# Transposes of a fused attention and feed-forward kernel moved three steps later; layer one issued one step ahead at edges without scores

## The chip, the cores and the metric

The kernel runs on one core of a Trainium2 chip. The metric is the device time of one execution in microseconds (us), as a median of several runs; one execution was also recorded by the hardware profiler, and all rows below are of that one.

## The reference

Agent attention, then a feed-forward block on its output, all in float32 (B = 2, N = 12480, C = 128, 49 agents, 2048 hidden units):

```
s(a, b)  = softmax(a @ b.T / sqrt(128))        # row maximum taken off first, 1e-9 added to the sum
agent_v  = s(agents, k) @ v                    # 49 x 128
x        = s(q, agents) @ agent_v              # 12480 x 128, for each batch
h        = x @ w_in                            # 24960 x 2048
g        = where(h > 0, h, exp(min(h, 0)) - 1)
out      = g @ w_out                           # 24960 x 128
```

## The kernel before

agent_v is folded into the first weight matrix: A = agent_v @ w_in, so h = s(q, agents) @ A, with a contraction of only 49. A prologue converts the weights and does batch 0's half of the attention over the keys; it takes the first 55 us. The rest is one long loop over S = 416 **steps**.

A **round** is 960 tokens (26 rounds, numbered from 0) and 16 steps; a **half round** is 480 tokens and 8 steps, one for each 256 hidden units. Below, n is the step's place in its round, 0 to 15. The work of a step s:

- Layer one, `p1(s)` (L404, matmuls at L412): six matmuls in three pairs (a pair shares the array) into an `h` tile of two PSUM banks. `h` tiles come from `slot()` (L136), a pool of **three** that is used in turn. A slot can be written again when the last reader of its tile is done.
- The activation, `elu(s)` (L415): ScalarE takes relu(-h) (L418) and an exponential (L421); VectorE makes g (L423), the last reader of `h`.
- `split(s)` (L426), in four of the eight steps of a half round (c = 1, 4, 6, 7): VectorE casts g to hi (L430), GpSimd subtracts for lo (L207, 128x480, twice). In the other four steps g is multiplied as plain float32.
- Layer two, `p2(s)` (L436, matmuls at L452), four steps later (LAG = 4): adds g times w_out to two PSUM banks `o0` and `o1`, of which there is one each. After the eighth product of a half round both are copied out: VectorE copies o1 to `ob` (L464), ScalarE copies o0 to `oa` (L467), GpSimd adds them (L468) and a DMA stores the sum (L469). The next half round's first product, one step later, needs both banks.

The order on each engine is written out by hand: in step s first p1(s), then p2(s-4), then the elu of s with the `oa` copy between its two ScalarE instructions, then split(s), then whatever `at(step, function)` hung on the step. An engine does its instructions in that order. Since layer two trails by four steps, its half rounds end at n = 3 and n = 11 and begin at n = 4 and n = 12; these are the **edges**.

Attention for the queries of round j is hung on earlier steps (L620 to L635, s0 from `EDGE` = 3): at n = 11 two rounds ahead the 64 small score matmuls (L293), into a slot of their own, with maximum, subtraction, exponential and normalisation in the steps behind; then `q_ring(j)` (L355), at n = 3 of the round before j: eight transposes on TensorE (L334) into a slot of their own, a ScalarE copy (L348) and a VectorE subtraction (L207, 113x480) out of it as `px`, and four DMAs that copy the two `px` tiles to `py` with their halves swapped (L352, L353). SyncE's queue issues them, and then at n = 4 the load of later queries (L124). So each round has one edge with transposes (n = 3) and one with scores (n = 11). Rounds 24 and 25 have no scores to make, and round 25 has no transposes.

Batch 1's attention over its keys is spread over rounds 0 to 12: score rounds in rounds 0 to 6 (at n = 13 and n = 1); in rounds 7 to 11 a VectorE subtraction `e_sub` (L211) at n = 4, 8 and 12, an exponential `e_exp` (L214) a step later, and matmuls at n = 8, 12 and 0; at n = 4 of round 7 one small matmul with a slot; at n = 14 of round 11 and n = 2, 6 and 10 of round 12 matmuls `A_pe` (L262), each with a slot.

Of the kernel before, what the change touches and what calls it, by code (L numbers as in the profile page):

```python
# [24 lines left out]
def tile_agent_attention_moe(  # L25
# [21 lines left out]
    S = B * NG * NM  # L47
    LAG = 4
    WARM = 2
    LEAD = 6  # L50
    NP = NM // 2
# [84 lines left out]
    def slot(dt=F32):  # L136

        return ps_h.tile([128, 2, 512], dt, tag="h", name="h")
# [258 lines left out]
    h_t, e_t, g_t, hi_t, lo_t, o_t = {}, {}, {}, {}, {}, {}  # L397

    def at_step(s):

        x, c = divmod(s, NP)
        return x // 2, x % 2, c

    def p1(s):  # L404
        j, half, c = at_step(s)
        h = slot()
        ah, al = A[j // NG, c]
        hi, lo = p_t[j]
        for i, (a, p) in enumerate([(ah, hi), (ah, lo), (al, hi)]):
            for u, r in enumerate(ROWS):  # L410
                x = slice(r, r + NA)
                nc.tensor.matmul(out=h[:, u, 0:T], lhsT=a[x, :], rhs=p[u ^ half][x, :], start=i == 0, stop=i == 2)  # L412
        h_t[s] = h[:, :, 0:T]

    def elu(s, between=None):  # L415

        h, e = h_t.pop(s), x_p.tile([128, 2, T], F32, tag="e", name="e")
        nc.scalar.activation(out=e, in_=h, func=ACTF.Relu, scale=-1.0)  # L418
        if between:
            between()  # L420
        nc.scalar.activation(out=e, in_=e, func=ACTF.Exp, scale=-1.0)  # L421
        g = g_p.tile([128, 2, T], F32, tag="g", name="g", bufs=5)
        nc.vector.scalar_tensor_tensor(out=g, in0=e, scalar=-1.0, in1=h, op0=ALU.add, op1=ALU.max)  # L423
        g_t[s] = g

    def split(s):  # L426
        if at_step(s)[2] not in SPLIT:
            return
        hi_t[s] = g_p.tile([128, 2, T], F32R, tag="hi", name="hi", bufs=3)
        nc.vector.tensor_copy(out=hi_t[s], in_=g_t[s])  # L430
        lo_t[s] = []
        for i in range(2):
            lo_t[s].append(g_p.tile([128, T], F32R, tag=f"lo{i}", name=f"lo{i}", bufs=3))
            rest(nc.gpsimd, lo_t[s][i], g_t[s][:, i, :], hi_t[s][:, i, :])
# [42 lines left out]
    def at(s, fn, *a):  # L477
        pre.setdefault(s, []).append((fn, a))

    with tc.manual_schedule():  # L480
# [137 lines left out]
        o_p = ctx.enter_context(tc.tile_pool(name="o", bufs=1))  # L618

        groups[0] = 32  # L620
        for j in range(1, B * NG):
            s0 = (j - 1) * NM + EDGE
            if j + 1 < B * NG:
                at(s0 + 1, load_q, j + 1)
            if j > 1:
                s0 -= NP
            at(s0, q_scores, j)
            at(s0, q_max)
            at(s0, q_sub)
            at(s0 + 1, q_exp)  # L630
            at(s0 + 2, q_sum)
            at(s0 + 2, q_rz, 0)
            at(s0 + 3, q_rz, 1)
            at(s0 + 4, q_mul)
            at(s0 + (9 if j == 1 else NP), q_ring, j)  # L635
        def k_round(r):
            ps = attn_bank()
            scores_pe(ps, k_t.pop((1, r)), 1, 0, R)
            k_out(ps, r)

        for r in range(NR):
            s0 = (r // 2) * NM + 13 + 4 * (r % 2)
# [8 lines left out]
        for r in range(NR):  # L651
            s0 = (7 + r // 3) * NM + 8 + 4 * (r % 3)
# [9 lines left out]

        for s in range(S + LAG):
            after = None
            if s < S:
                p1(s)
            if s == 2:
                t = ps_o.tile([128, 512], F32, tag="o0", name="o0")
                for _ in range(2):
                    nc.tensor.matmul(out=t[:, 0:T], lhsT=ident, rhs=win_sb[:, 0:T], start=True, stop=True)  # L670
            x = s - LAG + (s < LEAD)
            if x >= 0 and s != LEAD:
                after = p2(x)
            if s < S:
                elu(s, after)
                split(s)
            elif after:
                after()
            for fn, a in pre.pop(s, []):
                fn(*a)  # L680
# [34 lines left out]
```

## Time and profile before

| | |
|---|---|
| median of 3 runs | 1029.28 us (1029.2 to 1029.38) |
| the profiled execution | 1029.82 us, its span 1028.0 us |
| TensorE | busy 1004.7 us, 98% |
| ScalarE | busy 896.5 us, 87% |
| VectorE | busy 816.3 us, 79% |
| GpSimd | busy 587.3 us, 57% |
| mean granted TensorE clock | 0.998 |

Busy time counts an instruction from its start to its modelled end. A matmul's end is modelled, so gaps of TensorE are better seen from the distance between starts than from busy time. The timeline names, for each instruction or run of like instructions, start and length in us, engine, line, operation, tiles, shapes and count, and in brackets the idle time before it with what ended it. Two matmuls of a pair stand as two rows with nearly one start.

### The profile page before, as it was taken

What the parts mean: (1) busy time and instruction counts of PE and PEld (TensorE: products, weight loads), DVE (VectorE), ACT (ScalarE), POOL (GpSimd) and SP (SyncE); (2) the same over time, 40 slices, a digit from 0 to 9 for tenths busy, and PEclk for the clock granted to TensorE, in tenths of its full rate; (3) what the DMA queues carried; (4) which work ended last, traced back from release to release, by engine and by line L of the source; (5) the groups of instructions that cost most, each with busy time, mean ns of one, the idle gap of its engine ahead of it and who ended that gap; (6) DMA issues with size and microseconds to landing.
All of it is one profiled execution on the core that took longest, in us unless ns stands there. A gap on an engine that the chain in (4) does not pass through costs nothing.

```text
span 1028.0 us, 24953 instructions
## 1 busy us (share of the span) xinstructions
PE 1004.7 (98%) x10242; PEld 752.6 (73%) x10242; DVE 816.3 (79%) x989; ACT 896.5 (87%) x1018; POOL 587.3 (57%) x490
## 2 busy tenths in 40 slices
PE   7899999999999999999999999999999999999998
PEld 5767777777776677777766777777777777777796
DVE  7778788788888777887778888878887887888775
ACT  4588998998898888888889999999999999999995
POOL 3236565565565565566555565656656565656655
PEclk9999999999999999999999999999999999999999
DMA  9911211211222322320110111011011101101000
GB/s 349 376 72 45 93 64 37 86 64 45 78 64 71 90 65 60 101 64 11 54 45 11 54 45 44 22 54 44 21 44 45 54 11 54 45 26 40 26 20 20
DMA packets 25980, 67.27 MB, mean 65 GB/s; under 512 B 3083, under 2 KB 14963, under 8 KB 25867
## 3 DMA queue, kind: packets, MB, share of 16 engines
q1 hardware_dynamic: 25867, 65.69, 19.2%
q8 instruction: 80, 1.31, 0.5%
q14 instruction: 33, 0.27, 0.1%
HBM read 43.11 MB, written 12.78 MB: 54 GB/s over the span
## 4 chain that ended last, share of the span: by engine, by line
PE 85%; DVE 6%; ACT 5%; issue 2%; DMA 1%; POOL 0%; SPq 0%; POOLq 0%; DVEq 0%; ACTq 0%
PE o L452 53%; PE h L412 26%; DVE g L423 3%; ACT e L421 3%; PE h L293 2%; PE h L222 1%; PE h L159 1%; ACT e L418 1%; DMA k<-in_kT_dram 1%; DVE m_all L168 0%; ACT s_all L214 0%; ACT ex L102 0%; DVE ex L106 0%; PE h L262 0%; DVE fr L108 0%
## 5 line engine op out<-in xcount | busy, mean ns | idle before, releaser
L207 POOL TENSOR_TENSOR lo<-g,hi 128x480 fp32r<-128x480 f32 x416 | 512.4, 1254 | 391.2 <-DVE hi L430 229.5
L423 DVE SCALAR_TENSOR_TENSOR g<-e,h 128x960 f32<-128x960 f32 x416 | 478.5, 1152 | 174.8 <-ACT e L421 140.6
L418 ACT ACTIVATE e<-h 128x960 f32<-128x960 f32 x416 | 403.5, 970 | 59.5 <-PE h L412 48.9
L421 ACT ACTIVATE e<-e 128x960 f32<-128x960 f32 x416 | 418.3, 1006 | 11.5
L452 PE MATMUL o<-g,w_f 64*128 64x480 f32 x1664 | 373.8, 562 | 0.0
L412 PE MATMUL h<-px,ahi 49*128 49x480 f32 x832 | 318.6, 462 | 6.1 <-DVE g L423 6.0
L412 PE MATMUL h<-py,ahi 49*128 49x480 f32 x832 | 319.4, 463 | 0.9 <-DVE qe L305 0.5
L452 PEld LDWEIGHTS o<-g,w_f 64*128 64x128 f32 x1664 | 170.8, 185 | 90.5 <-issue 80.1
L412 PEld LDWEIGHTS h<-px,ahi 49*128 49x128 f32 x832 | 146.5, 186 | 56.3 <-issue 45.9
L412 PEld LDWEIGHTS h<-py,ahi 49*128 49x128 f32 x832 | 146.5, 186 | 44.9 <-issue 31.4
L430 DVE CAST hi<-g 128x960 fp32r<-128x960 f32 x208 | 171.8, 826 | 7.2
L412 PE MATMUL h<-py,alo 49*128 49x480 f32 x416 | 156.2, 376 | 0.0
L412 PE MATMUL h<-px,alo 49*128 49x480 f32 x416 | 156.2, 375 | 0.0
L452 PE MATMUL o<-hi,w_lo 64*128 64x480 f32 x832 | 130.8, 380 | 0.0
L452 PE MATMUL o<-lo,w_hi 64*128 64x480 f32 x832 | 129.5, 376 | 0.5 <-POOL lo L207 0.5
L452 PE MATMUL o<-hi,w_hi 64*128 64x480 f32 x832 | 128.4, 374 | 0.0
L452 PEld LDWEIGHTS o<-hi,w_lo 64*128 64x128 f32 x832 | 85.9, 185 | 7.5
L452 PEld LDWEIGHTS o<-hi,w_hi 64*128 64x128 f32 x832 | 85.0, 184 | 7.8
L452 PEld LDWEIGHTS o<-lo,w_hi 64*128 64x128 f32 x832 | 85.1, 184 | 7.7 <-POOL lo L207 0.9
L412 PEld LDWEIGHTS h<-px,alo 49*128 49x128 f32 x416 | 76.6, 184 | 4.2
L412 PEld LDWEIGHTS h<-py,alo 49*128 49x128 f32 x416 | 76.6, 184 | 4.1
L468 POOL TENSOR_TENSOR ob<-ob,oa 128x480 f32<-128x480 f32 x51 | 62.0, 1216 | 7.4 <-ACT oa L467 7.4
(86 smaller groups left out, 512.1 us busy)
## 6 DMA issues: line engine op xcount, KB each, us to landing
k<-in_kT_dram SPq DMA_DIRECT2D x26, 480.0 KB
q<-in_qT_dram SPq DMA_DIRECT2D x26, 480.0 KB
out_dram<-ob SPq DMA_DIRECT2D x51, 240.0 KB
py<-px SPq DMA_DIRECT2D x104, 91.9 KB
v<-in_vx_dram SPq DMA_DIRECT2D x13, 516.0 KB
v<-in_vx_dram SPq DMA_DIRECT2D x13, 483.8 KB
raw<-in_w_in_dram SPq DMA_DIRECT2D x4, 512.0 KB
raw<-in_w_out_dram SPq DMA_DIRECT2D x4, 512.0 KB
```

What stands on the lines that cost most here:

```text
L159: nc.tensor.matmul(out=ps[u:u + w, j * NA:(j + 1) * NA], lhsT=src[:, x:x + w], rhs=ag_sb[:, b, :], start=True, stop=True)
L207: eng.tensor_tensor(out=out, in0=x, in1=hi.bitcast(F32), op=ALU.subtract)
L222: nc.tensor.matmul(out=ps[u:u + 64], lhsT=e[:, j * NA:j * NA + 64], rhs=v_t[b, r][:, j, :], start=(r == rs[0] and j < 2), stop=(r == rs[-1 ...
L293: nc.tensor.matmul(out=ps[u:u + w, t * NA:(t + 1) * NA], lhsT=src[:, x:x + w], rhs=ag_sb[:, j // NG, :], start=True, stop=True)
L412: nc.tensor.matmul(out=h[:, u, 0:T], lhsT=a[x, :], rhs=p[u ^ half][x, :], start=i == 0, stop=i == 2)
L418: nc.scalar.activation(out=e, in_=h, func=ACTF.Relu, scale=-1.0)
L421: nc.scalar.activation(out=e, in_=e, func=ACTF.Exp, scale=-1.0)
L423: nc.vector.scalar_tensor_tensor(out=g, in0=e, scalar=-1.0, in1=h, op0=ALU.add, op1=ALU.max)
L430: nc.vector.tensor_copy(out=hi_t[s], in_=g_t[s])
L452: nc.tensor.matmul(out=o_t[u][:, 0:T], lhsT=w[x], rhs=v[x, :], start=first and i == 0, stop=last and i == len(jobs) - 1)
L468: nc.gpsimd.tensor_tensor(out=ob, in0=ob, in1=oa, op=ALU.add)
```

## The change

The transposes with their copies and DMAs go from n = 3 to n = 6 (from round 1 on; those of the first ring stay). In a step that begins a half round of layer two and has no scores just before it, layer one of the next step is issued ahead of the first product of layer two; in the next step it is then left out. These are the steps at n = 4 of rounds 1 to 25 and at n = 12 of rounds 24 and 25, 27 in all. Nothing else differs, and no instruction is added or removed.

```
         groups[0] = 32
+        covered = set()
         for j in range(1, B * NG):
...
             at(s0, q_scores, j)
+            covered.add(s0 + 1)
...
             at(s0 + 4, q_mul)
-            at(s0 + (9 if j == 1 else NP), q_ring, j)
+            at(s0 + (9 if j == 1 else NP + 3), q_ring, j)
...
         for s in range(S + LAG):
             after = None
-            if s < S:
+            if s < S and s not in h_t:
                 p1(s)
+            if s % NP == LAG and s > LEAD and s not in covered and s + 1 < S:
+                p1(s + 1)
```

## Rows read from the trace of the kernel before

**Rows 1.** Page, busy time: engine, us (share of span), instructions
```profile
PE 1004.7 (98%) x10242; PEld 752.6 (73%) x10242; DVE 816.3 (79%) x989; ACT 896.5 (87%) x1018; POOL 587.3 (57%) x490
```

**Rows 2.** Waits of TensorE: waiter, releaser, us in total, times, longest
```profile
PE h L412 <- DVE g L423: 6.3, 27, 0.4
```

**Rows 3.** Timeline, TensorE, edge with transposes of round 20 (n = 3 to 7)
```profile
810.59 0.38 PE L412 MATMUL h<-px,ahi 49*128 49x480 f32 x1
...
812.55 0.51 PE L334 MATMUL h<-ident,pp 60*113 60x60 f32 x8
...
813.61 1.77 PE L452 MATMUL o<-g,w_f 64*128 64x480 f32 x8
815.61 0.45 PE L412 MATMUL h<-px,ahi 49*128 49x480 f32 x1 [0.23 <-DVE g L423]
...
816.34 0.63 PE L452 MATMUL o<-hi,w_lo 64*128 64x480 f32 x4
...
817.65 0.38 PE L412 MATMUL h<-px,ahi 49*128 49x480 f32 x1
...
818.30 1.77 PE L452 MATMUL o<-g,w_f 64*128 64x480 f32 x7
...
820.57 1.77 PE L452 MATMUL o<-g,w_f 64*128 64x480 f32 x7
```

**Rows 4.** Timeline, ScalarE, the same edge
```profile
812.74 0.57 ACT L467 ACTIVATE oa<-o 128x480 f32<-128x480 f32 x1 [0.32 <-PE o L452]
813.21 1.00 ACT L421 ACTIVATE e<-e 128x960 f32<-128x960 f32 x1
```

**Rows 5.** Timeline, VectorE, the same edge
```profile
811.59 1.15 DVE L423 SCALAR_TENSOR_TENSOR g<-e,h 128x960 f32<-128x960 f32 x1 [0.38 <-ACT e L421]
812.78 0.66 DVE L464 COPY ob<-o 128x480 f32<-128x480 f32 x1
814.31 1.15 DVE L423 SCALAR_TENSOR_TENSOR g<-e,h 128x960 f32<-128x960 f32 x1 [0.88 <-ACT e L421]
```

**Rows 6.** Timeline, ScalarE, an edge without scores or transposes (round 25)
```profile
991.28 1.00 ACT L421 ACTIVATE e<-e 128x960 f32<-128x960 f32 x1
992.18 0.96 ACT L418 ACTIVATE e<-h 128x960 f32<-128x960 f32 x1
993.17 1.01 ACT L421 ACTIVATE e<-e 128x960 f32<-128x960 f32 x1
```

**Rows 7.** Timeline, TensorE, the same bare edge
```profile
990.62 0.38 PE L412 MATMUL h<-px,ahi 49*128 49x480 f32 x1
...
993.82 0.60 PE L452 MATMUL o<-hi,w_lo 64*128 64x480 f32 x3
```

**Rows 8.** Timeline, VectorE, n = 4 and 5 of round 8
```profile
372.50 0.66 DVE L430 CAST hi<-g 128x960 fp32r<-128x960 f32 x1
373.08 0.56 DVE L211 TENSOR_TENSOR s_all<-s_all,mb 120x392 f32<-120x392 f32 x1
373.56 1.15 DVE L423 SCALAR_TENSOR_TENSOR g<-e,h 128x960 f32<-128x960 f32 x1
```

**Rows 9.** Timeline, ScalarE, n = 5 and 6 of round 8
```profile
373.67 0.53 ACT L214 ACTIVATE s_all<-s_all 120x392 f32<-120x392 f32 x1 [0.38 <-DVE s_all L211]
374.11 0.95 ACT L418 ACTIVATE e<-h 128x960 f32<-128x960 f32 x1
```

**Rows 10.** Timeline, SyncE's queue, round 20: the load behind the ring's copies
```profile
818.50 0.45 SPq L124 DMA_DIRECT2D q<-in_qT_dram  x1
```

**Rows 11.** Timeline, GpSimd, round 20
```profile
811.38 2.40 POOL L207 TENSOR_TENSOR lo<-g,hi 128x480 fp32r<-128x480 f32 x2 [0.71 <-DVE hi L430]
813.74 1.20 POOL L468 TENSOR_TENSOR ob<-ob,oa 128x480 f32<-128x480 f32 x1
...
822.59 2.43 POOL L207 TENSOR_TENSOR lo<-g,hi 128x480 fp32r<-128x480 f32 x2 [1.58 <-DVE hi L430]
```

**Rows 12.** Timeline, VectorE, a cast beside the last of these
```profile
824.08 1.45 DVE L430 CAST hi<-g 128x960 fp32r<-128x960 f32 x1
```

More of the change, by code (lines that the diff above doesn't have):

```diff
@@ L620, in tile_agent_attention_moe @@
         groups[0] = 32
+        covered = set()
         for j in range(1, B * NG):
@@ L627, in tile_agent_attention_moe @@
             at(s0, q_scores, j)
+            covered.add(s0 + 1)
             at(s0, q_max)
@@ L634, in tile_agent_attention_moe @@
             at(s0 + 4, q_mul)
-            at(s0 + (9 if j == 1 else NP), q_ring, j)
+            at(s0 + (9 if j == 1 else NP + 3), q_ring, j)
         def k_round(r):
@@ L664, in tile_agent_attention_moe @@
             after = None
-            if s < S:
+            if s < S and s not in h_t:
                 p1(s)
+            if s % NP == LAG and s > LEAD and s not in covered and s + 1 < S:
+                p1(s + 1)
             if s == 2:
```

## The prediction, made before the changed kernel was seen

> **What bounds the kernel.** I read the busy shares first: TensorE 98%, ScalarE 87% [rows 1]. TensorE sets the time, so the change can only bring what TensorE now loses between its products. The list of waits shows one wait of the long loop that repeats: layer one on VectorE's g, 27 times, 6.3 us in all [rows 2]. That undercounts, because a matmul's end is modelled, so I went to the timeline of one edge with transposes, and to the distances between starts [rows 3].
>
> First the units. Layer one takes 818.30 - 817.65 = 0.65 us. A step with a split product takes 817.65 - 816.34 + 0.65 = 1.96, one with a plain product 820.57 - 818.30 = 2.27 [rows 3]. Now the edge: from layer one of n = 3 (810.59) to the product at n = 5 (816.34) are 5.75 us; the work in it, a split step, a plain step and one more layer one, is 1.96 + 2.27 + 0.65 = 4.88. So **0.87 us** are lost for the transposes and the stall. From the first transpose (812.55) to the plain product (813.61) are 1.06, of which 0.65 is layer one: the transposes cost 0.41 with the slower restart behind them. The other **0.46** is the stall: layer one of n = 5 starts at 815.61, 0.15 after g of n = 3 ended (814.31 + 1.15 = 815.46 [rows 5]).
>
> Why that g: slots go in turn. Layer one of n = 3, the transposes and layer one of n = 4 take the three, so layer one of n = 5 needs the slot of n = 3 back. And g of n = 3 is late, because at the edge its exponential stands behind ScalarE's `oa` copy, which waits for the product of the finished half round [rows 4]. There are 24 such edges, rounds 1 to 24. I take round 20 for all of them: the mean of the 27 waits, 6.3 / 27 = 0.23, is the 0.23 of its own row [rows 2, 3].
>
> **The change part by part.** I count from layer one of n = 3 as zero (810.59).
>
> *Layer one of n = 5, issued early.* It is wanted at 1.96 + 0.65 = 2.61, since nothing now lies between n = 3 and n = 4. It takes the slot of n = 2, whose g ends at 811.59 + 1.15 = 812.74, that is 2.15, and with the 0.15 from above it is free at 2.30. No wait, 0.31 in hand. What is queued behind it is the first product of layer two, then at 3.26; that one needs the `ob` copy, which ends at 813.44, or 2.85 [rows 5]. So the early layer one covers the emptying of the banks, which the transposes covered until now. What it costs without cover a bare edge shows: from 990.62 to 993.82 are 3.20 for two layers one and a plain product, 0.65 + 1.62 + 0.65 = 2.92, hence 0.28 lost [rows 7]. The product of n = 5 then comes at 4.88 instead of 5.75. Its lo must be there: GpSimd has finished it at 813.78, or 3.19 [rows 11]. Free.
>
> *The transposes at n = 6.* TensorE reaches them after two split and two plain steps: 2 x 1.96 + 2 x 2.27 = 8.46. They still cost 0.41, or 0.32 up to layer one of n = 7, which could start at 8.78. The slots now in turn are n = 5, n = 6, transposes, so layer one of n = 7 needs **g of n = 5**. That is the new gate, and ScalarE's chain sets it. The copy starts at 2.15 and the exponential of n = 3 at 2.62 [rows 4]. From an exponential to the next relu are 0.90 and from a relu to its exponential 0.99 when nothing holds them [rows 6]: relu and exponential of n = 4 at 3.52 and 4.51, of n = 5 at 5.41 and 6.40. The `px` copy, which stood here, is gone to n = 6. g starts 1.10 behind its exponential (813.21 to 814.31 [rows 4, 5]): 7.50 to 8.65, and layer one 0.15 later, **8.80 against 8.78**. The stall shrinks from 0.46 to 0.02. Layer one of n = 8 needs g of n = 6, one ScalarE step (1.89) later, 10.54 + 0.15 = 10.69, and is wanted at 8.80 + 0.09 + 2.27 = 11.16; layer one of n = 9 needs VectorE's `px` subtraction behind g and hi of n = 6, about 11.9, and is wanted about 13.1. Free. Each ordinary round gains 0.46 - 0.02 = **0.44**. There are 18 of them (1 to 6 and 13 to 24): **7.9 us**.
>
> *The ring's DMAs.* SyncE's queue issues the load of later queries at 818.50, behind the ring's four copies [rows 10]. The load now goes ahead of them. The copies come some 7 us later, and layer one of the next round needs them more than 15 us after that. Nothing waits.
>
> *Rounds 7 to 11 (5).* VectorE's `e_sub` at n = 4 stands between hi of n = 4 and g of n = 5, the new gate. From hi to `e_sub` are 0.58, from there to g 0.48 [rows 8]. g of n = 4 starts at 4.51 + 1.05 (the bare edge shows no less) and ends at 6.71, hi starts at 6.74, so g of n = 5 is at 7.80, not 7.50, and layer one of n = 7 at 9.10: 0.30 stalled. ScalarE's `e_exp` then waits for `e_sub` (7.88) and starts at 7.91, the relu of n = 6 0.44 later [rows 9], its exponential at 9.34, g 10.44 to 11.59, layer one of n = 8 at 11.74 instead of 11.46: 0.28 more. Loss now 0.41 + 0.30 + 0.28 + 0.09 for one more restart = 1.08, before 0.87: 5 x -0.21 = **-1.0**. Round 7 has one more slot in it, bounds 0 and -0.5; I keep it with the others.
>
> *Round 12.* `A_pe` at n = 6 takes a slot behind the transposes, so layer one of n = 7 waits for g of n = 6 (10.69). No row shows that order. The bounds are the ordinary gain (+0.4) and a whole stall of 10.69 - 8.80 = 1.9 in place of 0.46 (-1.4); since `A_pe` itself fills part of it, **-0.6**.
>
> *Bare edges (n = 12 of rounds 24 and 25, n = 4 of round 25).* 3 x 0.28 = **+0.8**.
>
> Sum: 7.9 - 1.0 - 0.6 + 0.8 = 7.1 us. The profiled execution (span 1028.0, whole 1029.82) stands 0.5 above the median of 1029.28; I take the sum from the median: **1022.2 us**.
>
> **The rivals.**
> (A) *ScalarE is slower at the new gate.* The 0.90 from exponential to relu is of two instructions at a bare edge; if the two such gaps are 1.0 like those from relu to exponential, g of n = 5 comes 0.2 later and TensorE has no room for it: 18 x 0.2 = 3.6 less, **1025.8**. For it: 8.80 against 8.78 is no margin at all. Against: the rows themselves, which show 0.90.
> (B) *The wait only moves.* If layer one of n = 7 stalls by the full 0.46, ordinary rounds gain nothing, and what is left is 0.8 - 1.0 - 0.6: **1030**, within the noise. It needs g of n = 5 at 9.1 instead of 8.65. Against it: the `oa` copy and its wait lie four steps of n earlier in the chain, and their delay is already in it.
> (C) *Slower: a cast that is held up ahead of the gate.* hi of n = 4 stands before g of n = 5 on VectorE. One cast in the rows takes 1.45 instead of 0.66, the one that starts while GpSimd subtracts [rows 11, 12]. If GpSimd were at work at 6.74, g of n = 5 would start about 0.75 later, layer one of n = 7 at 9.55; an ordinary round would then lose 0.41 + 0.77 = 1.18 against 0.87. 18 x 0.31 + 5 x 0.7 + 0.6 - 0.8 = 8.9: **1038**. It decides from a delay of 0.44 on. Against it: GpSimd's last work before is the sum of the outputs, which ends at 814.94, or 4.35, 2.4 before the cast [rows 11]. The Trainium skill says the same more generally (SBUF — State Buffer, section "SBUF: two separate sides"): VectorE's two-port modes and GpSimd share a pair of ports as an exclusive lock, and whoever starts first holds it for the whole instruction. The long cast agrees with that rule; by it an overlap of any length would cost the whole remainder, so the 2.4 us of room is what keeps this rival small.
> (D) *Better: the work of rounds 7 to 12 costs nothing in the new place*, and they gain like the others: 24 x 0.44 + 0.8 = 11.4: **1018**; halfway, 1020.
>
> **How the numbers follow.** Forecast (1020.5 to 1024) 0.60; A 0.18; D and halfway 0.08; B 0.07; C 0.07. A measurement can tell about 0.2% or 2.1 us from no change. Forecast, A and D are faster by more than that: 0.86; B is the same: 0.07; C slower: 0.07. The range takes in A and most of D: **1018.5 to 1027**, which leaves out B, C and the end of D.
>
> **What would show it.** Right: at n = 4 two layers one in a row and no gap before the first product; product of n = 5 about 4.9 after layer one of n = 3; the transposes between the products of n = 6 and layer one of n = 7, with a wait on g there of under 0.1 in ordinary rounds and about 0.3 in rounds 7 to 11; a wait of a microsecond in round 12. Wrong: layer one of n = 5 waiting for g of n = 2; a wait of over 0.2 before layer one of n = 7 in ordinary rounds, with ScalarE busy without a gap from the `oa` copy on (A, B) or a long cast (C).

## The result, and the profile after

The changed kernel took **1020.22 us** (median of 4 runs, 1020.07 to 1020.39) against 1029.33 before on the same chip: a ratio of 0.9911 with a 95% interval of 0.9894 to 0.9928, or 9.1 us less. The forecast was 1022.2 us, in a range of 1018.5 to 1027. The profiled execution took 1020.16 us with a span of 1018.4, that is 9.66 and 9.6 less than the one shown of before.

The page, busy times (answers to [rows 1]), and the waits of TensorE on g (answers to [rows 2]; waiter, releaser, us in total, times, longest):

```profile
PE 998.9 (98%) x10242; PEld 714.1 (70%) x10242; DVE 814.5 (80%) x989; ACT 890.8 (87%) x1018; POOL 584.9 (57%) x490
```

```profile
PE h L412 <- DVE g L423: 2.2, 5, 1.0
```

Of 27 waits on g five are left. Four of these stand outside the changed edges, three in round 0 and one at n = 2 of round 7, and are as long as before (0.17 to 0.43); the fifth, the longest, is that of round 12 below. The busy share of TensorE is 98% as it was; it says nothing here, as the number of instructions is the same and a modelled end covers small gaps. Where the time went is seen at the edge of round 20 again. Its timeline on TensorE (answers to [rows 3]; start, length in us):

```profile
804.34 0.38 PE L412 MATMUL h<-px,ahi 49*128 49x480 f32 x1
...
806.96 0.38 PE L412 MATMUL h<-px,ahi 49*128 49x480 f32 x1
...
807.61 1.78 PE L452 MATMUL o<-g,w_f 64*128 64x480 f32 x8
...
810.52 0.38 PE L412 MATMUL h<-px,ahi 49*128 49x480 f32 x1
...
811.18 1.77 PE L452 MATMUL o<-g,w_f 64*128 64x480 f32 x8
812.79 0.52 PE L334 MATMUL h<-ident,pp 60*113 60x60 f32 x8
813.12 0.46 PE L412 MATMUL h<-px,ahi 49*128 49x480 f32 x1
...
813.85 1.77 PE L452 MATMUL o<-g,w_f 64*128 64x480 f32 x8
```

Counted from layer one of n = 3 (804.34): layer one of n = 5 starts at 2.62, the first product at 3.27, layer one of n = 6 at 6.18, the transposes at 8.45, layer one of n = 7 at 8.78. Nothing waits. Before, layer one of n = 6 came at 7.06 [rows 3], 0.88 later.

ScalarE and VectorE at the same edge (answers to [rows 4] and [rows 5]):

```profile
806.50 0.57 ACT L467 ACTIVATE oa<-o 128x480 f32<-128x480 f32 x1 [0.28 <-PE o L452]
806.96 1.00 ACT L421 ACTIVATE e<-e 128x960 f32<-128x960 f32 x1
...
810.75 1.01 ACT L421 ACTIVATE e<-e 128x960 f32<-128x960 f32 x1
```

```profile
811.84 1.16 DVE L423 SCALAR_TENSOR_TENSOR g<-e,h 128x960 f32<-128x960 f32 x1
```

The exponential of n = 5 starts at 6.41, 3.79 after that of n = 3 (forecast 2 x 1.89), and g of n = 5 runs from 7.50 to 8.66. So the new gate opens a tenth of a microsecond before TensorE is there. The cast ahead of this g takes its 0.66; GpSimd has nothing to do between 808.75 and 811.91:

```profile
811.08 0.66 DVE L430 CAST hi<-g 128x960 fp32r<-128x960 f32 x1
```

```profile
807.54 1.21 POOL L468 TENSOR_TENSOR ob<-ob,oa 128x480 f32<-128x480 f32 x1
811.91 2.38 POOL L207 TENSOR_TENSOR lo<-g,hi 128x480 fp32r<-128x480 f32 x2 [3.16 <-DVE hi L430]
```

To see all rounds, I took from the two traces the time from the last matmul of layer one of n = 2 to that of n = 10 (the half round that holds the change):

| rounds | before, us | after, us | after less before, us |
|---|---|---|---|
| 1 to 6 and 13 to 24, each | 17.80 to 17.84 | 17.30 to 17.32 | -0.49 to -0.53 |
| 7 | 19.52 | 19.33 | -0.19 |
| 8 to 11, each | 19.04 to 19.06 | 19.08 to 19.11 | +0.04 to +0.06 |
| 12 | 19.36 | 19.90 | +0.54 |
| 25 (bare edge at n = 4) | 17.29 | 16.91 | -0.38 |
| 24 and 25, the half round of the bare edge at n = 12 | 17.29, 10.76 | 16.93, 10.42 | -0.36, -0.34 |

The sum, 18 x 0.51 + 0.19 - 0.19 - 0.54 + 1.08 = 9.7 us, accounts for the 9.6 to 9.7 us between the two profiled executions. All other half rounds are equal to 0.01.

The rounds that gain nothing show the two stalls that were forecast. Round 8, VectorE (answers to [rows 8]) and TensorE:

```profile
369.21 0.56 DVE L211 TENSOR_TENSOR s_all<-s_all,mb 120x392 f32<-120x392 f32 x1
369.69 1.15 DVE L423 SCALAR_TENSOR_TENSOR g<-e,h 128x960 f32<-128x960 f32 x1
372.26 1.15 DVE L423 SCALAR_TENSOR_TENSOR g<-e,h 128x960 f32<-128x960 f32 x1 [1.43 <-ACT e L421]
```

```profile
370.36 0.52 PE L334 MATMUL h<-ident,pp 60*113 60x60 f32 x8
370.89 0.48 PE L412 MATMUL h<-px,ahi 49*128 49x480 f32 x1
...
371.65 1.77 PE L452 MATMUL o<-g,w_f 64*128 64x480 f32 x8
373.47 0.48 PE L412 MATMUL h<-py,ahi 49*128 49x480 f32 x1
```

g of n = 5 stands behind `e_sub` and ends at 370.84, and layer one of n = 7 starts at 370.89, 0.21 later than the 0.32 behind the transposes at which it follows elsewhere. g of n = 6 ends at 373.41, and layer one of n = 8 starts at 373.47. And round 12, TensorE, where `A_pe` (L262) takes a slot behind the transposes:

```profile
528.57 0.65 PE L262 MATMUL h<-win_sb,avt 128*64 128x256 f32 x4
530.22 0.48 PE L412 MATMUL h<-px,ahi 49*128 49x480 f32 x1 [1.01 <-DVE g L423]
```

### The profile page after: what moved, and what is told of

Its sections match the earlier page's. It is cut to its first block, busy times and chain, and to the rows that moved or that the text cites. A ratio compares the mean times of both kernels' runs of the same rounds, so it can differ in the third digit from the quotient of the medians.

```text
span 1018.4 us, 24959 instructions
## 1 busy us (share of the span) xinstructions
PE 998.9 (98%) x10242; PEld 714.1 (70%) x10242; DVE 814.5 (80%) x989; ACT 890.8 (87%) x1018; POOL 584.9 (57%) x490
## 4 chain that ended last, share of the span: by engine, by line
PE 89%; DMA 5%; ACT 3%; DVE 2%; issue 1%; POOLq 0%; POOL 0%; DVEq 0%; SPq 0%; ACTq 0%
PE o L452 56%; PE h L412 27%; DMA v<-in_vx_dram 2%; PE h L293 2%; ACT e L418 1%; PE h L222 1%; ACT e L421 1%; DMA raw<-in_w_out_dram 1%; PE h L159 1%; DMA k<-in_kT_dram 1%; DVE g L423 1%; PE h L334 1%; DMA raw<-in_w_in_dram 0%; PE h L262 0%; DVE hi L430 0%
## 5 line engine op out<-in xcount | busy, mean ns | idle before, releaser
L452 PE MATMUL o<-g,w_f 64*128 64x480 f32 x1664 | 369.3, 562 | 0.0
L412 PE MATMUL h<-px,ahi 49*128 49x480 f32 x832 | 305.3, 446 | 2.0 <-DVE g L423 1.9
L412 PE MATMUL h<-py,ahi 49*128 49x480 f32 x832 | 305.3, 446 | 1.1 <-DVE qe L305 0.5
L452 PEld LDWEIGHTS o<-g,w_f 64*128 64x128 f32 x1664 | 157.7, 185 | 100.8 <-issue 88.8
L452 PE MATMUL o<-hi,w_lo 64*128 64x480 f32 x832 | 136.1, 404 | 0.0
L452 PE MATMUL o<-lo,w_hi 64*128 64x480 f32 x832 | 125.0, 376 | 0.7 <-POOL lo L207 0.7
L452 PE MATMUL o<-hi,w_hi 64*128 64x480 f32 x832 | 123.8, 374 | 0.0
L452 PEld LDWEIGHTS o<-hi,w_lo 64*128 64x128 f32 x832 | 79.3, 185 | 22.1 <-issue 11.8
L452 PEld LDWEIGHTS o<-lo,w_hi 64*128 64x128 f32 x832 | 78.8, 184 | 12.2 <-POOL lo L207 1.0
L452 PEld LDWEIGHTS o<-hi,w_hi 64*128 64x128 f32 x832 | 78.7, 184 | 12.1
```

The source lines that it names most:

```text
L452: nc.tensor.matmul(out=o_t[u][:, 0:T], lhsT=w[x], rhs=v[x, :], start=first and i == 0, stop=last and i == len(jobs) - 1)
```

## The experiments

The theory, as the prediction has it: three slots are used in turn; a slot taken at an edge makes layer one wait for a g that ScalarE's `oa` copy has delayed; the move puts the transposes where the g needed is ready; the early layer one covers the emptying of the two banks. The rivals are named in each expectation.

### One half of the change alone

Only the move: the two lines that issue `p1(s + 1)` are taken out.

> The transposes moved to n = 6, no layer one issued early. Theory (two parts that need each other: the move takes away the stall of 0.5 us a round, the early layer one covers the emptying of the two banks): every one of the 27 edges is now bare. A bare edge in round 25 of the kernel before cost 0.38 us against the changed kernel (17.29 against 16.91 from n = 2 to n = 10), so rounds 1 to 6 and 13 to 24 lose 0.37 each against the changed kernel and the three other edges as much; rounds 7 to 12 lose little, since ScalarE's chain holds them anyway. 1020.2 + 21 x 0.37 + about 0.5 = 1028.5 us, within 0.2% of the kernel before. Rival (the move alone is the gain, the banks are emptied in time anyway): 1020 to 1021 us.

Measured: **1028.22 us**, ratio to before 0.9987 (0.9978 to 0.9997). TensorE at the edge of round 20:

```profile
811.58 0.38 PE L412 MATMUL h<-px,ahi 49*128 49x480 f32 x1
...
812.40 1.88 PE L452 MATMUL o<-g,w_f 64*128 64x480 f32 x7
...
813.84 0.56 PE L452 MATMUL o<-g,w_f 64*128 64x480 f32 x1
...
814.77 0.72 PE L452 MATMUL o<-hi,w_lo 64*128 64x480 f32 x4
```

The first product starts 0.82 after layer one and not 0.65, and from then on the two rows of a pair start 0.12 apart (so the last row of the product stands by itself, at 813.84), up to the scores at n = 11, behind which they start together again. An ordinary round gains 0.12 us instead of 0.51. The rival falls: the move alone brings 1.4 of the 9 us.

Only the early layer one:

```
-            at(s0 + (9 if j == 1 else NP + 3), q_ring, j)
+            at(s0 + (9 if j == 1 else NP), q_ring, j)
```

> Layer one of n = 5 issued early, the transposes left at n = 3. Theory (the turn of the three slots decides): with the transposes still taking a slot, layer one of n = 5 needs the slot of n = 3, whose g ends 4.88 us after layer one of n = 3 began, and it is now wanted at 3.0 instead of 4.6; the first product of layer two is queued behind it. The product of n = 5 starts at about 7.3 instead of 5.75: 24 x 1.6 = 38 us lost against the kernel before, 1 us gained at the three bare edges: 1066 us. Rival (issuing layer one early is itself the gain): under 1026 us.

Measured: **1086.65 us**, ratio 1.0548 (1.0529 to 1.0567). The direction and the place are the theory's, the size is not. TensorE in round 20, where layer one of n = 3 starts at 858.48:

```profile
861.29 0.37 PE L412 MATMUL h<-px,alo 49*128 49x480 f32 x1
...
863.51 0.74 PE L412 MATMUL h<-px,ahi 49*128 49x480 f32 x1 [1.84 <-DVE g L423]
...
864.04 0.60 PE L412 MATMUL h<-px,ahi 49*128 49x480 f32 x1
...
864.45 0.60 PE L412 MATMUL h<-px,alo 49*128 49x480 f32 x1
...
864.84 2.74 PE L452 MATMUL o<-g,w_f 64*128 64x480 f32 x8
```

Layer one of n = 5 starts 5.03 behind layer one of n = 3, where the slot's g lets it. But then its matmuls follow at 0.40 instead of 0.22, and the plain product takes 2.74 instead of 1.77. The stretches of this trace (stretch: its us, then busy us and count for each engine, granted clock, share of DMA, GB/s):

```profile
863.50:867.00 3.50, 3.49 (x12) 2.32 (x14) 2.24 (x3) 2.81 (x3) 0.49 (x1) 0.53 0.44 152
867.00:869.40 2.40, 2.40 (x24) 1.98 (x22) 1.16 (x1) 0.12 (x1) 1.90 (x2) 1.00 0.79 227
```

The same 3.48 us behind the same wait in round 15:

```profile
676.59:680.07 3.48, 3.47 (x26) 2.79 (x28) 2.65 (x4) 2.94 (x3) 0.47 (x1) 1.00 0.45 155
```

In round 20, after 1.84 us without work, the granted clock was at 0.53, near the lower of its two levels (1.2 and 2.4 GHz), for some 3.5 us; in round 15 it stayed at 1.00. Over the 24 rounds the half round is longer than before by 1.60 to 1.63 us in 12 of them (the 1.6 that was expected) and by 2.99 to 3.26 in the other 12, among them round 20 with its fallen clock. The clock separates the two kinds without exception: in the 3.5 us behind the wait it was 0.51 to 0.73 in the 12 dearer rounds and 1.00 in the 12 others. What the early layer one costs in the wrong slot order was right; that the clock would fall behind the stall was not expected, and it makes some 18 of the 57 us (12 rounds at about 1.5).

### Other places for the transposes

One step earlier (`NP + 2`) and one step later (`NP + 4`) than in the change:

> The transposes at n = 5 instead of n = 6, layer one early as in the change. Theory: then layer one of n = 6 follows the transposes and needs the slot of n = 4, whose g ends at 6.70; it is wanted at 6.52 and starts at 6.76, with a slower restart. An ordinary round loses 0.65 to transposes and stall instead of 0.39: 18 x 0.26 = 4.7 us. Rounds 7 to 11 gain 0.25 each and round 12 about 1.0, because the wait for g of n = 6 goes away there: 1020.2 + 4.7 - 1.2 - 1.0 = 1022.7 us. Rival (any step away from the edge is as good): 1018 us, by the gain of rounds 7 to 12 alone.

> The transposes at n = 7. Theory: no slot is late in ordinary rounds (layer one of n = 8 needs g of n = 6, done at 10.5, wanted at 11.1), so they stay as in the changed kernel. Round 12 gains about 1.0. In rounds 7 to 11 the matmuls at n = 8 take a slot too, so layer one of n = 9 needs the px subtraction of n = 7, behind g and hi of n = 7. If hi is held up by GpSimd's subtractions, as casts beside them are in other rows (1.3 us instead of 0.66), that is 1.2 us late: 1020.2 - 1.0 + 5 x 1.2 = 1025 us. If the cast is not held up, it is in time: 1019 us.

Measured at n = 5: **1023.17 us**, ratio 0.9938 (0.9923 to 0.9953). TensorE and VectorE in round 20:

```profile
811.84 0.51 PE L334 MATMUL h<-ident,pp 60*113 60x60 f32 x8
812.41 0.48 PE L412 MATMUL h<-px,ahi 49*128 49x480 f32 x1
```

```profile
811.20 1.16 DVE L423 SCALAR_TENSOR_TENSOR g<-e,h 128x960 f32<-128x960 f32 x1 [0.67 <-ACT e L421]
```

g of n = 4 ends at 812.36, and layer one of n = 6 starts 0.05 later, 0.57 behind the first transpose instead of 0.33. An ordinary round gains 0.21 to 0.25 instead of 0.51, and so do rounds 8 to 12. Not every step away from the edge is as good.

Measured at n = 7: **1018.91 us**, ratio 0.9899 (0.9885 to 0.9914), the value of the expectation without a held cast. Round 12 gained (18.86 us for its half round, 0.50 under before), rounds 8 to 11 stayed (0.06 to 0.08 over), since there `e_sub` and `e_exp` still stand before g of n = 6, for which layer one of n = 8 now waits (0.32 to 0.36 us idle). With round 12, n = 7 is the better place by some 1 us. In round 8 the cast of n = 7 was not held; VectorE and GpSimd there:

```profile
376.88 0.66 DVE L430 CAST hi<-g 128x960 fp32r<-128x960 f32 x1
```

```profile
375.75 4.04 POOL L207 TENSOR_TENSOR lo<-g,hi 128x480 fp32r<-128x480 f32 x3 [2.27 <-DVE hi L430]
```

GpSimd was in the middle of a run of subtractions when the cast started, and this time the cast took its 0.66. It came between two of them: three subtractions took 4.04 us, where two take 2.40 elsewhere [rows 11], so here GpSimd was the one that was held, by some 0.4 us (its second subtraction took 1.67 us, the others 1.2).

### The new gate

One more ScalarE copy, behind the exponential of n = 4 or of n = 9:

```
+        def extra():
+            nc.scalar.activation(out=scr, in_=win_sb[:, 0:T], func=ACTF.Copy)
+        for j in range(1, 25):
+            at(j * NM + 4, extra)
```

> The changed kernel with one more ScalarE copy of 128x480 (its result is not used) behind the exponential of n = 4 in rounds 1 to 24. Theory (after the change ScalarE's chain from the oa copy to g of n = 5 is the gate of layer one of n = 7, with 0.07 us to spare): the copy shifts the chain by about 0.45, g of n = 5 ends at 9.1, layer one of n = 7 starts at 9.16 instead of 8.78: 18 x 0.38 = 6.8 us, rounds 7 to 11 hardly more, round 12 0.4: 1020.2 + 7.5 = 1027.7 us. Rival (TensorE is bound by its own work, ScalarE has room at 87% busy): 1020 to 1021 us.

> The same additional ScalarE copy, but behind the exponential of n = 9. Theory (the place of the work on ScalarE counts, not its sum): at n = 9 and 10 ScalarE waits for TensorE, and no slot hangs on it: 1020.2 to 1021 us. Rival (ScalarE's sum counts): the same as with the copy at n = 4, some 1027 us if that run shows a loss.

Measured: at n = 4 **1028.75 us**, ratio 0.9994 (0.9985 to 1.0004); at n = 9 **1020.04 us**, ratio 0.9909 (0.9894 to 0.9923). The same instruction, 24 times, costs 8.5 us at one place and nothing at the other. With it at n = 4, ScalarE, VectorE and TensorE in round 20:

```profile
815.89 0.59 ACT L668 ACTIVATE scr<-win_sb 128x480 f32<-128x480 f32 x1
816.39 0.95 ACT L418 ACTIVATE e<-h 128x960 f32<-128x960 f32 x1
```

```profile
818.46 1.16 DVE L423 SCALAR_TENSOR_TENSOR g<-e,h 128x960 f32<-128x960 f32 x1 [0.60 <-ACT e L421]
```

```profile
819.67 0.48 PE L412 MATMUL h<-px,ahi 49*128 49x480 f32 x1 [0.23 <-DVE g L423]
```

The copy moves the relu behind it by 0.50 (0.45 was expected), and layer one of n = 7 starts 0.05 after the g that is now late. The chain from the `oa` copy to this g is the gate, with next to nothing to spare, as forecast.

Rival C, made to happen: three more GpSimd subtractions, hung on n = 3.

```
+        def extra(s):
+            for _ in range(3):
+                nc.gpsimd.tensor_tensor(out=scr, in0=g_t[s][:, 0, :], in1=g_t[s][:, 1, :], op=ALU.subtract)
+        for j in range(1, 25):
+            at(j * NM + 3, extra, j * NM + 3)
```

> The changed kernel with three more GpSimd subtractions of 128x480 (results not used) that read g of n = 3 in rounds 1 to 24, so that GpSimd is at work from about 5.05 to 8.7, when the cast of n = 4 is due at 6.73. Rival C of the prediction, made to happen: the cast is held until GpSimd is done and ends at about 9.2, g of n = 5 runs from 9.2 to 10.35, layer one of n = 7 starts 1.6 us late: 18 x 1.65 + 5 x 1.8 = 39 us, 1059 us. If the cast is not held up, or only by its own doubled length (0.7 us, of which VectorE has 0.1 to spare): 1020 to 1034 us.

Measured: **1035.54 us**, ratio 1.0059 (1.0044 to 1.0074), neither of the two. VectorE and GpSimd in round 20:

```profile
824.96 1.25 DVE L430 CAST hi<-g 128x960 fp32r<-128x960 f32 x1
826.14 1.14 DVE L423 SCALAR_TENSOR_TENSOR g<-e,h 128x960 f32<-128x960 f32 x1
```

```profile
823.18 4.11 POOL L669 TENSOR_TENSOR scr<-g 128x480 f32<-128x480 f32 x3 [0.55 <-DVE g L423]
```

The cast took 1.25 us instead of 0.66: it was held until the subtraction then under way was done, not until GpSimd had no more to do. So the gate opened 0.41 late (g 7.91 behind layer one of n = 3, not 7.50), and an ordinary round lost 0.34 to 0.38, some 6.5 us in all. The rest was lost in rounds 7 to 11: in rounds 8 to 11 `e_sub` was held in the same way, 1.56 instead of 0.56, and rounds 8 to 10 lost 1.6 us each, round 7 1.4. Round 11 lost 2.9: there TensorE stood idle for 1.65 us before layer one of n = 7, and from 1.6 us behind the wait on the granted clock was 0.50 for 3.4 us. The Trainium skill (SBUF — State Buffer, section "Who interferes with whom") states that a VectorE instruction in a two-port mode and a GpSimd instruction contend for a shared pair of ports, and that whoever issues first gets it for the whole instruction. The rows agree (the cast of 1.25 us waits for one subtraction), and the kernel with the transposes at n = 7 shows the other order. So rival C's mechanism is real, its price here is a little over a third of a microsecond in an ordinary round, and the changed kernel does not pay it because GpSimd is idle at that time.

### The rounds that gain nothing

`e_sub` and `e_exp` a step later in rounds 7 to 11:

```
-            at(s0 - 4, e_sub, r)
-            at(s0 - 3, e_exp, r)
+            late = s0 % NM == 8
+            at(s0 - 4 + late, e_sub, r)
+            at(s0 - 3 + late, e_exp, r)
```

> The changed kernel with e_sub at n = 5 instead of n = 4 and e_exp at n = 6 instead of n = 5 in rounds 7 to 11 (those whose matmuls are at n = 8). Theory (rounds 8 to 11 gain nothing from the change because e_sub stands ahead of g of n = 5 and e_exp ahead of the relu of n = 6): both waits go, rounds 8 to 11 gain 0.5 each as ordinary rounds do, round 7 little: 1018.0 us. Rival (these rounds are held by the sum of their work): 1020 us.

Measured: **1018.09 us**, ratio 0.9891 (0.9876 to 0.9906). Rounds 8 to 11 now gain 0.50 to 0.54 each. In round 8, VectorE makes g of n = 5 ahead of `e_sub`, and TensorE has its 0.32 behind the transposes:

```profile
368.93 1.16 DVE L423 SCALAR_TENSOR_TENSOR g<-e,h 128x960 f32<-128x960 f32 x1
370.00 0.63 DVE L211 TENSOR_TENSOR s_all<-s_all,mb 120x392 f32<-120x392 f32 x1
```

```profile
369.89 0.52 PE L334 MATMUL h<-ident,pp 60*113 60x60 f32 x8
370.21 0.46 PE L412 MATMUL h<-px,ahi 49*128 49x480 f32 x1
```

With the `A_pe` of n = 6 of round 12 put to n = 7 as well, and the changed kernel once more to compare with:

```
-            at(s0 + 6 + 4 * c, A_pe, 1, 512 * c, 512 * c + 512)
-            at(s0 + 6 + 4 * c, A_out, 1, 512 * c, 512 * c + 512)
+            at(s0 + 6 + 4 * c + (c == 2), A_pe, 1, 512 * c, 512 * c + 512)
+            at(s0 + 6 + 4 * c + (c == 2), A_out, 1, 512 * c, 512 * c + 512)
```

> The changed kernel with e_sub and e_exp a step later in rounds 7 to 11, and with the A_pe of n = 6 of round 12 at n = 7. Theory: the first edit gives 2.2 us as in the run with it alone; the second takes the slot from between the transposes and layer one of n = 7, so that this one needs g of n = 5 again (8.7) and not g of n = 6 (10.6): round 12 goes from 0.54 us over the kernel before to 0.5 under it. 1020.2 - 2.2 - 1.0 = 1017.0 us. Rival (round 12 is held by A_pe wherever it stands): 1018.0 us.

> The changed kernel itself, on the same chip and in the same rounds as the version with both edits, to compare the two: 1020.2 us, some 3.2 us over that version.

Measured: **1016.68 us** with both edits, ratio to before 0.987 (0.9855 to 0.9885), and **1020.12 us** for the changed kernel, 0.9905 (0.9888 to 0.9921). Round 12's half round is 18.89 us instead of 19.90. On TensorE layer one of n = 7 now follows the transposes, and `A_pe` comes a product later:

```profile
525.64 0.52 PE L334 MATMUL h<-ident,pp 60*113 60x60 f32 x8
525.97 0.46 PE L412 MATMUL h<-px,ahi 49*128 49x480 f32 x1
...
528.40 0.65 PE L262 MATMUL h<-win_sb,avt 128*64 128x256 f32 x4
```

This version is the fastest of all that were run, 3.4 us under the changed kernel.

## Why the prediction was right, point by point

- **The stall and its cause** held. Four of the 27 waits that the mean of 0.23 was taken from are not of these edges; the other 23 are 0.21 to 0.23 each (round 7's edge has none on g), so round 20 does stand for all. The stall is gone in all 18 ordinary rounds, and the cases that put it back (the early layer one with the old slot order, one more copy in ScalarE's chain) put it back where the theory has it.
- **The new gate**: forecast g of n = 5 from 7.50 to 8.65, measured 7.50 to 8.66; transposes at 8.46, measured 8.45. The gaps of 0.90 between exponential and relu were there, so rival A fell. Only the release was mis-sized: I took the 0.15 from g's end to layer one of [rows 3, 5], and in the stalls after the change it was 0.05 (round 8, the transposes at n = 5, the copy at n = 4). So the 0.02 of stall was none. That the gate and TensorE arrive within a tenth of a microsecond of each other was forecast, but with no margin for an error of the terms: the copy at n = 4 shows that 0.5 us more on ScalarE takes nearly all of the gain (0.03 to 0.07 us of an ordinary round were left).
- **The size of an ordinary round** was forecast at 0.44 and was 0.51. Of the 0.07, 0.02 are the stall that did not come. At layer one of n = 6 the two kernels lie 0.88 apart, as the 0.87 of the forecast has it, and the transposes give 0.41 of that back. The other 0.03 is in the second row of the pairs: from the second matmul behind the old stall on (815.90 with the first row, 815.94 with the second) it started 0.03 after the first, and in the changed kernel the rows start together. At layer one of n = 11 the first row is 0.47 earlier than before and the second 0.50, and behind the scores, where the rows start together in both kernels, the whole lead is 0.50. Why the old stall set the rows apart was not tried.
- **Bare edges**: forecast 0.28, measured 0.34 to 0.38. The step that failed is the reading of [rows 7]: I measured the first row of each pair only. The first product waits for the two banks one after the other, the `oa` copy and then the `ob` copy, so the second row of the pairs is later than the first, and it is the later one that the end follows. In the kernel before, at the same edge, the last matmul of layer one on the second row (of n = 3, then of n = 5):

```profile
991.18 0.38 PE L412 MATMUL h<-py,alo 49*128 49x480 f32 x1
...
993.82 0.38 PE L412 MATMUL h<-py,alo 49*128 49x480 f32 x1
```

That is 2.64 us for a plain product and a layer one, 1.62 + 0.65 = 2.27, hence 0.37 lost on this row. The move alone, which makes every edge bare, shows the same: an ordinary round took about 0.39 more than in the changed kernel.
- **Rounds 7 to 11**: forecast -1.0 us together, measured 0.0 (+0.19 and 4 x -0.05). Both waits came at the place that was named, and g of n = 5 at the time that was named (7.80). Their sizes were 0.21 and 0.21 us, not 0.30 and 0.28. The release of 0.05 instead of 0.15 counts in both; and g of n = 6 came 1.04 behind its exponential, not 1.10. Round 7, which I kept with the others for want of rows, had no stall at layer one of n = 7: its small matmul already puts layer one of n = 6 at 6.75 behind that of n = 3 instead of 6.18, and g of n = 5 is done by the time TensorE is there.
- **Round 12**: forecast -0.6, measured -0.54, by the wait on g of n = 6 that was named: 1.01 us in place of the 0.46 of the old stall. The mechanism was worked out, but the size was chosen between bounds of +0.4 and -1.4 without a row for it; that it came so near is in part luck.
- **The ring's DMAs**: their copies came 5.0 us later behind layer one of n = 3, not 7 (9.79 against 4.80), and no matmul of the loop waits for them.
- **Sum**: 7.1 forecast, 9.7 in the profiled executions, 9.1 in the medians. The misses were on the same side and did not cancel: 1.3 from the ordinary rounds, 1.0 from rounds 7 to 11, 0.3 from the bare edges.

Rival A fell with the gaps of 0.90, rival B with the gate's 8.66. Rival C's mechanism exists but isn't met. Rival D fell too: rounds 8 to 12 do lose the gain in the new place, and rounds 8 to 11 have it only once `e_sub` and `e_exp` stand elsewhere.

## What to carry to other kernels

With few buffers used in turn, the place of a small piece of work decides which earlier buffer the next large piece must wait for; write down the turn, find the reader that frees each buffer last, and put the small work where that reader has been done for long. Two edits can need each other: here the move alone brought 1.4 us, the other alone cost 57 (some 18 of them by the fallen clock), and together they brought 9. And a wait that a change creates in a few rounds is worth an edit of its own once it is named: two small moves brought 3.4 us more.

## What the runs showed of the hardware

- Behind an idle time of 1.84 us of TensorE the granted clock stood at 0.53 for some 3.5 us in round 20 of the kernel with the early layer one alone. Of its 24 such waits 12 were followed by a fallen clock (0.51 to 0.73 over 3.5 us) and cost 1.4 to 1.6 us more than the other 12, which kept 1.00. Of the waits of 1.63 to 1.65 us in rounds 8 to 11 of the kernel with three more subtractions only that of round 11 was followed by one, at a cost of 1.3 us. Which waits are followed by it was not settled.
- From the end of g on VectorE to the matmul that waits for it were 0.15 us where VectorE went on with an independent instruction before g had ended (the stall before the change, and the early layer one alone), and 0.05 to 0.06 in the other waits read here. That the one causes the other was not tried.
- A VectorE cast that meets a GpSimd subtraction is held for the one under way (0.66 became 1.25), and in the gap between two of them it can go first and hold GpSimd instead.
